# Transposing later batches' attention scores by DMA in 16-bit halves, with a rearranged start, in a cross-covariance attention and MLP kernel

**Chip, cores, metric.** One NeuronCore of a Trainium2 chip. The metric is the device time of one execution in microseconds (us).

## The reference

```python
B, N, C = (4, 6080, 256)                      # q, k, v: fp32
qn = q / (np.linalg.norm(q, axis=1, keepdims=True) + 1e-06)
kn = k / (np.linalg.norm(k, axis=1, keepdims=True) + 1e-06)
s = kn.transpose(0, 2, 1) @ qn / tau           # 256 x 256 a batch
a = softmax(s, axis=-1)                        # (cut)
x = (v @ a).reshape(B * N, C)                  # 24320 x 256
h = x @ w_in                                   # w_in: 256 x 2048
out = gelu_tanh(h) @ w_out                     # w_out: 2048 x 256
```

The kernel folds `a @ w_in` into one matrix `aw` a batch. After that each row of `v` goes through `hp = v @ aw`, a gelu and `yp = g @ w_out`.

## The kernel before

A batch is 12 blocks of up to 512 rows, and a block is 8 steps, called slots here: so 96 slots a batch. In a slot TensorE makes four `hp` products and, after the first block, six to eight `yp` products of the block before. VectorE copies finished `yp` from PSUM, TensorE's output memory, to the tile `ysb`; this copy is called an eviction here. The attention of the next batch is fed in between as a generator, one piece a slot:

```python
for blk in range(n_blocks):
    vT = vT_of.pop(nb)
    turn_v(nb + 2)          # SyncE: transposes v of block nb+2 by DMA, 4 transposes of 64 KB
    load_v(nb + 3)          # GpSimd: loads v of block nb+3, casting fp32 to bf16
    for i in range(NP):     # NP = 8 slots
        # 4 products hp <- vT, aw ; gelu on ScalarE ; yp products of the block before
        next(fill, None)    # a piece of the next batch's attention
```

The generator ends each batch with the part that the change touches. Every `yield` ends a slot:

```python
norms(r)
Gs = scaled(G, r)           # VectorE, 128 x 2 x 256 fp32, scores with k's side scaled
yield
yield
T = turned(Gs)              # TensorE: 4 fp32 transposes into PSUM
# ... (cut) th = tanh(T * rh) on ScalarE, then per half jc:
for jc in range(2):
    yield
    # VectorE: den = 1 - th; den = 1 / den; eT = (1 + th) * den   = exp
yield
yield
rsinv = row_sums(eT)        # TensorE "rs", then a reciprocal on VectorE
for fs in range(D // 512):
    for ic in range(2):
        aw_part(eT, rsinv, aw_next, fs, ic)
        yield
```

Before the main loop the weights are loaded by SyncE and cast by GpSimd, with the loads of v for blocks 1 and 2 among them:

```python
for half in range(2):
    # ... (cut) w_in half: DMA, two casts
    load_v(1 + half)
for half in range(2):
    # w_out half: DMA, one cast (1.9 us)
```

Of the kernel before, what the change touches and what calls it, by code (L numbers as in the profile page):

```python
# [7 lines left out]

FP32 = mybir.dt.float32
BF16 = mybir.dt.bfloat16  # L10
AF = mybir.ActivationFunctionType
ALU = mybir.AluOpType
EPS = 1e-6
# [5 lines left out]
def kernel(  # L19
# [10 lines left out]
    nc = tc.nc  # L30
# [19 lines left out]
    split = ctx.enter_context(tc.tile_pool(name="split", bufs=1))  # L50
    accp = ctx.enter_context(tc.tile_pool(name="accp", bufs=1))
    smx = ctx.enter_context(tc.tile_pool(name="smx", bufs=2))
# [40 lines left out]
    n_all = S_ALL + 1  # L93


    first_chunks = chunks_of([12, 12, 5, 6, 4, 4, 2, 2], 2)
    TAIL, SHARED = 4, 6
    fillers = [0, 0, 5, 7, 4, 3, 1, 0]
    staged = []

    def halves(pool, tag, dtype, size, most=SMAX):
# [27 lines left out]
    ident = const.tile([128, 128], FP32)  # L129
# [68 lines left out]
                                 rhs=ident, is_transpose=True)  # L198
        return T

    def row_sums(eT):
        rs = pA.tile([128, 512], FP32, tag="a", name="rs")
        for ic in range(2):
            for jc in range(2):
                nc.tensor.matmul(
                    rs[:, ic : ic + 1],
                    lhsT=eT[:, jc, ic * 128 : ic * 128 + 128],
                    rhs=ones_bf,
                    start=jc == 0, stop=jc == 1)
        rsinv = smx.tile([128, 2], FP32, tag="rsinv", name="rsinv")  # L210
        nc.vector.reciprocal(rsinv, rs[:, 0:2])
        return rsinv
# [43 lines left out]
    for n, ch in enumerate(first_chunks):  # L256
        st, whole = staged[n]
        size = ch[1]
        qkb, qk_whole = halves(qkp, "qk", BF16, size)
        sqb, sq_whole = halves(sqp, "sq", BF16, size)  # L260
        hi = size + ch[2]
        if whole is None:
            todo = list(zip(qkb, sqb, st))
        else:
            todo = [[y[:, :, 0:hi] for y in (qk_whole, sq_whole, whole)]]
        for to, sq, x in todo:
            nc.vector.tensor_copy(to, x)  # L267
            if n != n_chunks - 2:
                nc.scalar.activation(sq, x, AF.Square)  # L269
        if n == n_chunks - 2:  # L270
            nc.scalar.activation(sqb[1][:, 0:hi], st[1][:, 0:hi], AF.Square)
            nc.vector.tensor_mul(sqb[0][:, 0:hi], qkb[0][:, 0:hi], qkb[0][:, 0:hi])
        keep_clock(fillers[n])
        for s, rows in slots_of(ch, 128):
            gram(G, qkb, s, rows, seen == 0, seen == n_all - 1)
            seen += 1
        if waiting is not None:
            pairs_of(*waiting)
            waiting = None
        if n < 2:  # L280
            pairs_of(n, sqb)
        elif n < TAIL:
            waiting = (n, sqb)
        else:
            sums_of([[y[:rows, s, :] for y in sqb] for s, rows in slots_of(ch, 128)], n == n_chunks - 1)

        for x in ((2, 3) if n == 0 else (4, 5) if n == 1 else (n + 4,)):
            stage_chunk(x)

    v0 = stage.tile([128, 2, SMAX, 256], FP32, tag="st", name="v0")  # L290
# [58 lines left out]
    for half in range(2):  # L349
        w = flat_stage(2)  # L350
        for x in range(2):
            c0 = half * 1024 + x * 512
            nc.sync.dma_start(out=w[:, :, x * 512 : x * 512 + 512], in_=win_v[:, :, c0 : c0 + 512])
            nc.gpsimd.tensor_copy(win_bf[:, :, c0 : c0 + 512], w[:, :, x * 512 : x * 512 + 512])
        load_v(1 + half)
    for half in range(2):
        w = flat_stage(8)
        nc.sync.dma_start(out=w, in_=wout_v[:, half * 8 : half * 8 + 8, :])
        nc.gpsimd.tensor_copy(wout_bf[:, half * 8 : half * 8 + 8, :], w)  # L359


    r = smx.tile([128, 4], FP32, tag="r", name="r")
# [3 lines left out]
    Gs = scaled(G, r)  # L366
# [6 lines left out]
                             rhs=ident, is_transpose=True)  # L373
        vps.append(p)
    keep_clock(1, pY, "y")
    T = turned(Gs)
    keep_clock(1, pY, "y")
    vT0 = vts.tile([128, 2, 512], BF16, tag="vT", name="vT")
    nc.vector.tensor_copy(vT0[:, 0, :], vps[0])
    eT = smx.tile([128, 2, 256], BF16, tag="eT", name="eT")  # L380
    aw = awp.tile([128, 2, D], BF16, tag="aw", name="aw")
    for jc in range(2):
        nc.scalar.activation(eT[:, jc, :], T[:, jc, :], AF.Exp, scale=r[:, jc : jc + 1])  # L383
    nc.scalar.activation(vT0[:, 1, :], vps[1], AF.Copy)


    firsts = []

    def first_aw(n, jc, pool=pY, tag="y"):

        if jc == 0:
            firsts.append(pool.tile([128, 512], FP32, tag=tag, name="ps"))
        nc.tensor.matmul(
            firsts[n][:, 0:256],
            lhsT=eT[:, jc, n % 2 * 128 : n % 2 * 128 + 128],
            rhs=win_bf[:, jc, n // 2 * 256 : n // 2 * 256 + 256],
            start=jc == 0, stop=jc == 1)

    first_aw(0, 0)
    first_aw(1, 0)  # L400
    rsinv = row_sums(eT)
    first_aw(0, 1)
    first_aw(1, 1)
    for n in (2, 3):
        first_aw(n, 0, pA, "a")
        first_aw(n, 1)
    for n in range(4):
        ic, lo = n % 2, n // 2 * 256
# [3 lines left out]
        else:  # L412
            nc.vector.tensor_scalar_mul(dst, firsts[n][:, 0:256], scale)  # L413
    nc.scalar.activation(dummy, ones_f, AF.Gelu_apprx_tanh)
    aw_left = [(fs, ic, *((pA, "a") if fs == 2 else (pY, "y"))) for fs in range(1, 4) for ic in range(2)]

    def more_aw(n):
        for _ in range(n):
# [18 lines left out]
    def attention_steps(b, aw_next):  # L437

        for n in range(16):
            if n in (3, 9):  # L440
                load_qk(b, n // 6)
            if b == 1 and n == 5:
                turn_v_on_pe(1)
            yield
        G = pA.tile([128, 2, 256], FP32, tag="a", name="G")
        acc = accp.tile([128, 2, 256], FP32, tag="acc", name="acc")
        seen = 0
        for n, ch in enumerate(later_chunks):
            load_qk(b, n + 2)
            qk, whole = loaded_of.pop((b, n))  # L450
            for s, rows in slots_of(ch, 128):
                first, last = seen == 0, seen == n_all - 1
                gram(G, qk, s, rows, first, last)
                flat = whole[:rows, :, s, :]
                if first:
                    nc.vector.tensor_mul(acc, flat, flat)
                else:
                    sq = sq1.tile([128, 2, 256], BF16, tag="sq", name="sq")
                    nc.vector.tensor_mul(sq[:rows], flat, flat)  # L459
                    nc.vector.tensor_add(acc[:rows], acc[:rows], sq[:rows])  # L460
                seen += 1
                yield
                if seen % 8 == 0:
                    yield


        parts = [split.tile([128, 2, 256], BF16, tag=f"part{n}", name="part") for n in range(3)]
        nc.vector.tensor_copy(parts[0], acc)
        nc.vector.tensor_sub(acc, acc, parts[0])
        nc.vector.tensor_copy(parts[1], acc)  # L470
        nc.vector.tensor_sub(parts[2], acc, parts[1])
        yield
        yield
        cols = pA.tile([128, 512], FP32, tag="a", name="cols")
        for n, part in enumerate(parts):
            col_sums(cols, [part[:, x] for x in range(2)], ones_bf, n == 0, n == 2)
        r = smx.tile([128, 4], FP32, tag="r", name="r")
        nc.vector.tensor_copy(r, cols[:, 0:4])  # L478
        nc.gpsimd.tensor_tensor(r, r, half4, op=ALU.pow)  # L479
# [4 lines that stand above are left out]
        rh = smx.tile([128, 2], FP32, tag="rh", name="rh")  # L484
        nc.vector.tensor_scalar_mul(rh, r[:, 0:2], 0.5)
        Gs = scaled(G, r)
        yield
        yield
        T = turned(Gs)
        eT = smx.tile([128, 2, 256], BF16, tag="eT", name="eT")  # L490
        if abs(inv_tau) > TANH_MAX:
            for jc in range(2):
                nc.scalar.activation(eT[:, jc, :], T[:, jc, :], AF.Exp, scale=r[:, jc : jc + 1])
            yield
        else:
            th = smx.tile([128, 2, 256], FP32, tag="th", name="th")
            den = smx.tile([128, 2, 256], FP32, tag="den", name="den")
            for jc in range(2):
                nc.scalar.activation(th[:, jc, :], T[:, jc, :], AF.Tanh, scale=rh[:, jc : jc + 1])
            for jc in range(2):  # L500
                yield
                nc.vector.tensor_scalar(den[:, jc, :], th[:, jc, :], -1.0, 1.0,
                                        op0=ALU.mult, op1=ALU.add)
                nc.vector.reciprocal(den[:, jc, :], den[:, jc, :])
                nc.vector.scalar_tensor_tensor(
                    out=eT[:, jc, :], in0=th[:, jc, :], scalar=1.0, in1=den[:, jc, :],
                    op0=ALU.add, op1=ALU.mult)
            yield
            yield
        rsinv = row_sums(eT)  # L510
# [4 lines that stand above are left out]
# [159 lines left out]
```

## Time and profile before

| | before |
|---|---|
| time, median of the runs beside the changed kernel | 753.86 us (753.45 to 754.20, 6 runs) |
| span of the profiled run | 752.0 us |
| TensorE busy | 726.4 us, 97% |
| wait for the first chunk of q and k | 15.8 us |
| TensorE's other waits, all together | 1.7 us |

TensorE is the bound from the moment that batch 0's `aw` is ready (first `hp` at 40.06 us) to the end. A line of the order of time has start, length, engine, source line, operation, output and inputs, count; in brackets the idle time before it and what ended it. In the names, `G` are the products of k and q (the scores), `Gs` the scaled and `T` the transposed scores, `th`, `den` and `eT` the steps of the exponential, `rs` its row sums, `vb` and `vT` a block of v as loaded and transposed. The lines of the page and of the waits are in the prediction below.

### The profile page before, as it was taken

The page shows a single profiled execution, that of the slowest core. Times are in us where ns is not written, and L with a number is a line of the kernel's source. Part 1 is how long each engine was busy: PE and PEld are TensorE (multiplying, and loading weights), DVE is VectorE, ACT ScalarE, POOL GpSimd, SP SyncE. Part 2 cuts the span into 40 slices and gives each one's busy share as a digit, 9 for nine tenths or more (in the row PEclk, how much of TensorE's full clock was granted, in tenths as well). Part 3 has the DMA queues.
Part 4 walks back from the last instruction along what each step waited for, and adds up shares of the span by engine and source line. Part 5 has one row for each costly group of instructions (what it writes and reads, how often), then busy time and mean ns, then how long its engine had stood idle before and what let it go on. Part 6 is the DMA issues. An engine that isn't in the chain of part 4 may idle for free.

```text
span 752.0 us, 12341 instructions
## 1 busy us (share of the span) xinstructions
PE 726.4 (97%) x5186; PEld 502.3 (67%) x5274; DVE 284.3 (38%) x497; ACT 420.3 (56%) x411; POOL 80.8 (11%) x154
## 2 busy tenths in 40 slices
PE   2899999999999999999999999999999999999998
PEld 1656766776666766776666666776666666666666
DVE  3733556463501646554521265555351011011011
ACT  4875555556456555555555555555645655555552
POOL 1061111101012102101001102010101000000000
PEclk9999999999999999999999999999999999999999
DMA  9989685613237685824325876671413533322111
GB/s 369 400 205 200 104 150 139 132 43 69 70 72 144 114 163 108 164 63 75 71 57 117 141 119 124 150 143 46 69 43 85 105 85 70 69 75 54 41 57 57
DMA packets 80183, 85.69 MB, mean 114 GB/s; under 512 B 55424, under 2 KB 59136, under 8 KB 79616
## 3 DMA queue, kind: packets, MB, share of 16 engines
q0 software_dynamic: 14480, 30.87, 25.7%
q1 hardware_dynamic: 65344, 52.39, 24.4%
q10 hardware_dynamic: 304, 1.64, 0.5%
q8 instruction: 41, 0.67, 0.4%
q14 instruction: 14, 0.11, 0.0%
HBM read 78.91 MB, written 24.90 MB: 138 GB/s over the span
## 4 chain that ended last, share of the span: by engine, by line
PE 94%; DMA 3%; ACT 1%; issue 1%; DVE 0%; POOL 0%; SPq 0%; DVEq 0%; POOLq 0%
PE yp L528 44%; PE hp L602 43%; PE G L158 4%; PE ps L218 2%; ACT sq L269 1%; DMA st<-in_q_dram 1%; DMA st<-in_k_dram 1%; PE T L196 0%; POOL wout_bf L359 0%; PE yp L633 0%; PE cols L170 0%; DVE qk L267 0%; DVE aw L413 0%; DVE Gs L188 0%; ACT eT L383 0%
## 5 line engine op out<-in xcount | busy, mean ns | idle before, releaser
L606 ACT ACTIVATE g<-hp 128x1024 bf16<-128x1024 f32 (+1 forms) x384 | 389.8, 1015 | 307.0 <-PE hp L602 295.2
L528 PE MATMUL yp<-wout_bf,g 128*128 128x256 bf16 x3024 | 392.0, 273 | 1.6 <-POOL wout_bf L359 0.7
L602 PE MATMUL hp<-vT,aw 128*128 128x512 bf16 (+1 forms) x1456 | 383.9, 377 | 3.8 <-DVE aw L413 0.2
L528 PEld LDWEIGHTS <-g 128*128 128x128 bf16 x3024 | 295.9, 98 | 114.3 <-issue 1.2
L602 PEld LDWEIGHTS <-aw 128*128 128x128 bf16 x1536 | 149.9, 98 | 104.1 <-DVE aw L413 0.5
L545 DVE COPY ysb<-yp 128x512 f32<-128x512 f32 (+1 forms) x95 | 64.9, 683 | 396.5 <-PE yp L528 396.5
L460 DVE TENSOR_TENSOR acc<-acc,sq 128x512 f32<-128x512 f32 x141 | 97.6, 692 | 4.8
L459 DVE TENSOR_TENSOR sq<-qkb 128x512 bf16<-128x512 bf16 x141 | 58.9, 418 | 0.0
L158 PE MATMUL G<-qkb 128*128 128x256 bf16 x288 | 55.0, 273 | 0.0
L307 POOL DMA_DIRECT2D vb<-in_v_dram x47 | 25.9, 552 | 88.6 <-DMA vT<-vb 81.3
L227 DVE TENSOR_SCALAR aw<-ps,rsinv 128x512 bf16<-128x512 f32 x30 | 22.4, 749 | 23.5 <-PE ps L218 18.3
L158 PEld LDWEIGHTS <-qkb 128*128 128x128 bf16 x288 | 28.2, 98 | 3.3
L332 POOL CAST gate<-g 1x1 f32<-1x1 bf16 x24 | 5.9, 245 | 227.8 <-ACT g L606 227.8
L158 PE MATMUL G<-qk 128*128 128x256 bf16 x96 | 13.5, 298 | 15.8 <-DVE qk L267 15.8
L269 ACT ACTIVATE sq<-st 128x3072 bf16<-128x3072 f32 (+2 forms) x9 | 21.1, 2379 | 11.1 <-DMA st<-in_q_dram 8.2
L158 PEld LDWEIGHTS <-qk 128*128 128x128 bf16 x96 | 9.8, 106 | 19.1 <-DVE qk L267 16.6
L267 DVE CAST qk<-st 128x3072 bf16<-128x3072 f32 (+2 forms) x10 | 14.2, 1438 | 13.1 <-DMA st<-in_q_dram 10.0
L218 PE MATMUL ps<-win_bf,eT 128*128 128x512 bf16 x54 | 16.4, 379 | 0.2
L479 POOL TENSOR_TENSOR r<-r,half 128x4 f32<-128x4 f32 x3 | 3.1, 1042 | 103.4 <-DVE r L478 103.4
L82 POOL DMA_DIRECT2D qkb<-in_q_dram x24 | 12.9, 537 | 5.8 <-issue 4.3
L585 POOL COPY g<-gr 128x1024 bf16<-128x1024 bf16 x2 | 2.1, 1036 | 101.3 <-PE yp L528 101.3
L82 POOL DMA_DIRECT2D qkb<-in_k_dram x24 | 12.9, 539 | 0.0
(73 smaller groups left out, 109.0 us busy)
## 6 DMA issues: line engine op xcount, KB each, us to landing
out_dram<-ysb SPq DMA_DIRECT2D x44, 512.0 KB, 3.0
vb<-in_v_dram POOLq DMA_DIRECT2D x43, 256.0 KB, 6.2
qkb<-in_q_dram POOLq DMA_DIRECT2D x21, 384.0 KB, 4.6
qkb<-in_k_dram POOLq DMA_DIRECT2D x21, 384.0 KB, 6.4
st<-in_q_dram SPq DMA_DIRECT2D x2, 1536.0 KB, 11.8
vT<-vb SPq DMA_TRANSPOSE x184, 3.0
wst<-in_moe_w_in_dram SPq DMA_DIRECT2D x4, 512.0 KB, 7.5
wst<-in_moe_w_out_dram SPq DMA_DIRECT2D x2, 1024.0 KB, 11.7
```

The lines of the kernel that those rows point to most:

```text
L82: engines[x].dma_start(out=dst[x][:, 0:size, :], in_=src[b, s0 * 128 : (s0 + size) * 128, :].rearrange("(p s) c -> p s c", s=size))
L158: nc.tensor.matmul(G[:, ic, :], lhsT=qk[1][:rows, s, ic * 128 : ic * 128 + 128], rhs=qk[0][:rows, s, :], start=first and ic == 0, stop=las ...
L218: nc.tensor.matmul(ps, lhsT=eT[:, jc, ic * 128 : ic * 128 + 128], rhs=win_bf[:, jc, fs * 512 : fs * 512 + 512], start=jc == 0, stop=jc == 1)
L227: nc.vector.tensor_scalar_mul(dst, ps, scale)
L269: nc.scalar.activation(sq, x, AF.Square)
L307: nc.gpsimd.dma_start(out=t[:, 0:n, :], in_=v_rows[r0 : r0 + n * 128, :].rearrange("(p s) c -> p s c", s=n))
L459: nc.vector.tensor_mul(sq[:rows], flat, flat)
L460: nc.vector.tensor_add(acc[:rows], acc[:rows], sq[:rows])
L528: nc.tensor.matmul(yp[:rows, at, :], lhsT=g[:, fc, s * 128 : s * 128 + rows], rhs=wout_bf[:, fc, :], start=fc == 0, stop=fc == FC - 1)
L545: nc.vector.tensor_copy(ysb[:, s0 : s + 1, :], yp[:, 0 : s + 1 - s0, :])
L602: nc.tensor.matmul(hp[:, j, :cols], lhsT=aw[:, cc, fc * 128 : fc * 128 + 128], rhs=vT[:, cc, :cols], start=cc == 0, stop=cc == 1)
L606: nc.scalar.activation(g[:, 2 * i : 2 * i + 2, :cols], hp[:, :, :cols], AF.Gelu_apprx_tanh)
```

## The change

The intent is to take the fp32 transposes of the scores of batches 1 to 3 off TensorE, to start the first products earlier, and to let w_out arrive before v of block 2. `first_chunks` are the pieces in which q and k of batch 0 are loaded, in units of 128 rows; `fillers` counts useless products ahead of each piece, which keep TensorE busy. The core of the diff:

```diff
-    first_chunks = chunks_of([12, 12, 5, 6, 4, 4, 2, 2], 2)
-    TAIL, SHARED = 4, 6
-    fillers = [0, 0, 5, 7, 4, 3, 1, 0]
+    first_chunks = chunks_of([2, 12, 12, 5, 6, 4, 2, 2, 2], 3)
+    TAIL, SHARED = 4, 7
+    fillers = [0, 0, 0, 5, 7, 4, 1, 1, 0]
@@ (cut: other PSUM pools for batch 0's row sums and first products; its T in two tiles)
-        load_v(1 + half)
+        if half == 0:
+            load_v(1)
     for half in range(2):
         w = flat_stage(8)
         nc.sync.dma_start(out=w, in_=wout_v[:, half * 8 : half * 8 + 8, :])
         nc.gpsimd.tensor_copy(wout_bf[:, half * 8 : half * 8 + 8, :], w)
+    load_v(2)
@@ (in the generator)
-        yield
-        yield
-        T = turned(Gs)
+        apart = split.tile([128, 2, 2, 256], U16, tag="apart", name="apart")
+        crossed = split.tile([128, 2, 2, 256], U16, tag="crossed", name="crossed")
+        T = split.tile([128, 2, 256], FP32, tag="T", name="T")
+        bits = Gs.bitcast(U16).rearrange("p a (j h) -> p h a j", h=2)
+        for h in range(2):
+            nc.vector.tensor_copy(apart[:, h], bits[:, h])
+            for ic in range(2):
+                nc.sync.dma_start_transpose(
+                    out=crossed[:, h, :, ic * 128 : ic * 128 + 128], in_=apart[:, h, ic, :])
+        for _ in range(6):
+            yield
+        bits = T.bitcast(U16).rearrange("p a (i h) -> p h a i", h=2)
+        for h in range(2):
+            nc.vector.tensor_copy(bits[:, h], crossed[:, h])
+        yield
```

More of the change, by code (lines that the diff above doesn't have):

```diff
@@ L10 @@
 BF16 = mybir.dt.bfloat16
+U16 = mybir.dt.uint16
 AF = mybir.ActivationFunctionType
@@ L199, in turned, with row_sums @@
         return T
-    def row_sums(eT):
-        rs = pA.tile([128, 512], FP32, tag="a", name="rs")
+    def row_sums(eT, rs=None):
+        if rs is None:
+            rs = pA.tile([128, 512], FP32, tag="a", name="rs")
         for ic in range(2):
@@ L267 @@
             nc.vector.tensor_copy(to, x)
-            if n != n_chunks - 2:
+            if n not in (n_chunks - 3, n_chunks - 2):
                 nc.scalar.activation(sq, x, AF.Square)
-        if n == n_chunks - 2:
+        if n in (n_chunks - 3, n_chunks - 2):
             nc.scalar.activation(sqb[1][:, 0:hi], st[1][:, 0:hi], AF.Square)
@@ L279 @@
             waiting = None
-        if n < 2:
+        if n < 3:
             pairs_of(n, sqb)
@@ L285 @@
             sums_of([[y[:rows, s, :] for y in sqb] for s, rows in slots_of(ch, 128)], n == n_chunks - 1)
-        for x in ((2, 3) if n == 0 else (4, 5) if n == 1 else (n + 4,)):
+        for x in ((2,) if n == 0 else (3, 4) if n == 1 else (5, 6) if n == 2 else (n + 4,)):
             stage_chunk(x)
@@ L375 @@
     keep_clock(1, pY, "y")
-    T = turned(Gs)
-    keep_clock(1, pY, "y")
+    T = [pY.tile([128, 512], FP32, tag="y", name="T") for _ in range(2)]
+    for ic in range(2):
+        for jc in range(2):
+            nc.tensor.matmul(T[jc][:, ic * 128 : ic * 128 + 128],
+                             lhsT=Gs[:, ic, jc * 128 : jc * 128 + 128],
+                             rhs=ident, is_transpose=True)
     vT0 = vts.tile([128, 2, 512], BF16, tag="vT", name="vT")
@@ L382, with first_aw @@
     for jc in range(2):
-        nc.scalar.activation(eT[:, jc, :], T[:, jc, :], AF.Exp, scale=r[:, jc : jc + 1])
+        nc.scalar.activation(eT[:, jc, :], T[jc][:, 0:256], AF.Exp, scale=r[:, jc : jc + 1])
     nc.scalar.activation(vT0[:, 1, :], vps[1], AF.Copy)
     firsts = []
-    def first_aw(n, jc, pool=pY, tag="y"):
+    def first_aw(n, jc, pool=pA, tag="a"):
         if jc == 0:
@@ L400 @@
     first_aw(1, 0)
-    rsinv = row_sums(eT)
+    rsinv = row_sums(eT, pH.tile([128, 2, 512], FP32, tag="h", name="rs")[:, 0, :])
     first_aw(0, 1)
@@ L404 @@
     for n in (2, 3):
-        first_aw(n, 0, pA, "a")
+        first_aw(n, 0, pY, "y")
         first_aw(n, 1)
@@ L414 @@
     nc.scalar.activation(dummy, ones_f, AF.Gelu_apprx_tanh)
-    aw_left = [(fs, ic, *((pA, "a") if fs == 2 else (pY, "y"))) for fs in range(1, 4) for ic in range(2)]
+    aw_left = [(fs, ic, *((pA, "a") if fs == 1 else (pY, "y") if fs == 2 else (pA, "a"))) for fs in range(1, 4) for ic in range(2)]
     def more_aw(n):
@@ L486, in attention_steps @@
         Gs = scaled(G, r)
+        apart = split.tile([128, 2, 2, 256], U16, tag="apart", name="apart")
[4 more added lines that the diff above has]
+            nc.vector.tensor_copy(apart[:, h], bits[:, h])
+            for ic in range(2):
+                nc.sync.dma_start_transpose(
[5 more added lines that the diff above has]
+            nc.vector.tensor_copy(bits[:, h], crossed[:, h])
         yield
-        yield
-        T = turned(Gs)
         eT = smx.tile([128, 2, 256], BF16, tag="eT", name="eT")
@@ L495, in attention_steps @@
         else:
-            th = smx.tile([128, 2, 256], FP32, tag="th", name="th")
-            den = smx.tile([128, 2, 256], FP32, tag="den", name="den")
+            th = split.tile([128, 2, 256], FP32, tag="th", name="th")
+            den = split.tile([128, 2, 256], FP32, tag="den", name="den")
             for jc in range(2):
```

## The prediction

> **What bounds the kernel now.** I read the page first (engine shares, slices, costliest groups), then TensorE's waits, then the order of time around the three places that the change touches: the start, the transposes of the scores, and the loads between 36 and 70 us. The page:
>
> ```profile
> PE 726.4 (97%) x5186; PEld 502.3 (67%) x5274; DVE 284.3 (38%) x497; ACT 420.3 (56%) x411; POOL 80.8 (11%) x154
> ...
> PE   2899999999999999999999999999999999999998
> ...
> DMA  9989685613237685824325876671413533322111
> ```
>
> TensorE is full in every slice but the first; the other engines have room. The DMA queues are full in the first three slices (to about 56 us) and then never again for long. TensorE's waits, all of them:
>
> ```profile
> PE G L158 <- DVE qk L267: 15.8, 3, 14.4
> PE yp L528 <- POOL wout_bf L359: 0.7, 1, 0.7
> PE T L196 <- DVE Gs L188: 0.4, 1, 0.4
> PE ps L393 <- ACT eT L383: 0.4, 1, 0.4
> PE hp L602 <- DVE aw L413: 0.2, 1, 0.2
> ```
>
> (Columns: who, on whom, total us, times, longest.) 15.8 us is the wait for the first chunk of q and k; the rest is small. After 52 us TensorE never waits: any TensorE work taken away there is gained one to one, and any new wait there is lost one to one. One step ("slot") of the main loop after the first block is four hp products and eight yp products; one slot of the second batch with the transposes of the scores in it, from the order of time:
>
> ```profile
> 181.56 1.03 PE L602 MATMUL hp<-vT,aw 128*128 128x512 bf16 x4
> ...
> 183.30 0.60 PE L196 MATMUL T<-ident,Gs 128*128 128x128 f32 x4
> ...
> 183.73 1.03 PE L602 MATMUL hp<-vT,aw 128*128 128x512 bf16 x3
> ...
> 185.47 1.03 PE L602 MATMUL hp<-vT,aw 128*128 128x512 bf16 x4
> ```
>
> From hp to hp it is 183.73-181.56 = 2.17 us with the four transposes and 185.47-183.73 = 1.74 without: they cost 0.43 us a batch, less than their busy time of 0.60, which overlaps.
>
> The first phase, to 34 us, is the load of q and k of batch 0 (2 x 6080 x 256 x 4 bytes = 12.45 MB) at the 400 GB/s of the slices; the windows of 2 us show the DMA share at 0.96 or more from 4 us to 48 us. The start of the steady part:
>
> ```profile
> 48.90 13.50 SPq L321 DMA_TRANSPOSE vT<-vb  x8
> ...
> 49.88 1.90 POOL L359 CAST wout_bf<-wst 128x2048 bf16<-128x2048 f32 x1 [2.02 <-PE hp L602]
> ...
> 51.72 0.54 POOL L307 DMA_DIRECT2D vb<-in_v_dram  x1
> ```
>
> GpSimd casts the second half of w_out at 49.88, and TensorE waits 0.7 us for it. The queue of SyncE transposes v of block 2 from 48.90 on (four transposes, 1.3 us each to issue), then v of block 3. Last, what a transpose by DMA takes from issue to landing, for those issued in 48 to 50.5 us, and in 57 to 62 us:
>
> ```profile
> vT<-vb SPq DMA_TRANSPOSE x2, 2.4
> ```
>
> ```profile
> vb<-in_v_dram POOLq DMA_DIRECT2D x3, 256.0 KB, 8.6
> ...
> vT<-vb SPq DMA_TRANSPOSE x4, 9.1
> ```
>
> The same 64 KB transposes take 2.4 us on an idle queue and 9.1 when GpSimd's casting loads are in flight. Over the whole run the median is 3.0.
>
> **What the Trainium skill says.** "DMA: Bandwidth & Descriptors", section "DMA Transpose (X-bar)": a transpose by DMA is for 2-byte types and is issued from SyncE or ScalarE only. Hence the split of the fp32 scores into upper and lower halves; the trace has v transposed this way from SyncE, 184 times. The same page, "Issuing engines are not separate DMA queues": DMAs of all issuers run on the same 16 engines and interleave. The trace agrees, with the 2.4 us that become 9.1. "TensorE: Matmul & The Clock Gate", Part 1: about 3.4 us without work put TensorE's clock back to half, and it takes as long to recover. The trace of before shows the recovery after the first wait: 24 G products took 4.50 us at 14.38, the next 24 took 2.79 us, a loss of 1.7.
>
> **The change part by part.**
>
> 1. Chunks 2, 12, 12, 5, 6, 4, 2, 2, 2 instead of 12, 12, 5, 6, 4, 4, 2, 2. The first squares and products start at about 5 us instead of 10.9 and 14.4. This gains nothing: the last k chunk (issued 25.61, in use at 34.4) lands when 12.45 MB have passed a full queue. ScalarE squares 1.5 MB in 2.75 us, faster than the 3.75 us that they take to arrive, so no backlog is worked off either. I put 0, at most 0.3 either way.
>
> 2. Scores of batch 0 in two PSUM tiles, first products and row sums in other pools. The exponential of the first half need not wait for the last transpose: about (0.74-0.27)/3 = 0.16 us. The row sums no longer share a pool with the first products, which hides little. Gain 0.15.
>
> 3. The load of v for block 2 goes behind the casts of w_out. Its 0.52 MB no longer compete with w_out: 0.52 MB at 400 GB/s = 1.3 us. The second half of w_out (issued 36.91, 12.9 us to landing, so 49.8) comes at 48.5, and its cast ends at 50.4 instead of 51.8. TensorE's wait of 0.7 us goes, and 0.2 of an earlier one. Gain 0.9. But the load of that v, issued at 42.68 and landed 6.2 us later (48.9), is now issued at 50.4. See rival A.
>
> 4. Batches 1 to 3: four fp32 transposes less on TensorE: 3 x 0.43 = 1.3 us gained. In their place VectorE makes 4 copies of 512 16-bit elements a batch, at 0.43 to 0.69 us (casts and copies of 128x512 in the trace), and SyncE issues 4 transposes at 1.3 us. Timing for batch 1: scaled scores ready at 182.0, the two halves split at 182.5 and 183, transposes issued at 182.5 to 187.7, while SyncE has nothing else until 188. No load is in flight (the next is after 204), so the last lands 2.4 us after its issue, near 189. Six slots of 1.74 after slot 75 VectorE gets to the merge, at 188 to 190; it waits a microsecond at most, and its next eviction is due at 191 or later. Off the path. Everything behind it shifts by five slots, and the last aw product goes from step 89 to step 94 of 96, so it still fits before the batch ends.
>
> Sum without anything new: -0.15 - 0.9 - 1.3 = -2.35, so 751.5 us.
>
> **The rivals.**
>
> A: a new wait, for v of block 2. The v load issued at 50.4 takes at least the 4.0 us of the fastest such load seen (at 176.06), so its transposes are issued at 54.4, 55.7, 56.9, 58.2. By then the loads of v of blocks 3 to 5 and of the first two chunks of q and k are in flight. In before, a transpose issued at 52.81 with fewer of them took 8.7 us, the four at 57.36 to 61.15 a median of 9.6, and the v load at 57.88 took 11.1 and landed at 69.0. With one load more in the same stretch, I estimate the fourth transpose to land between 67 and 70. Block 2's first hp ran at 64.84 in before and is due at 64.84 - 1.05 = 63.8. TensorE would stand for some 3 to 6 us, once. If it stands for over 3.4 us, the clock falls and costs about 1.7 more. Middle: 5 + 1.7 - 2.35 = +4.4, so 758 us. For it: every transpose of before that was issued in loaded stretches landed late. Against it: whoever tuned the kernel moved this load on purpose, and if these transposes go ahead of the backlog (2.4 us each) the last lands at 60.6 and nothing waits.
>
> B: the merge blocks VectorE. If the score transposes land late, VectorE stands at the merge, yp evictions are late and TensorE with them. Before shows 5.4 us for a transpose beside two v loads (176.5), but those loads land before 182. At most 1 us a batch: 754 without A.
>
> C: the gain is hidden altogether, because the slot is bound by something else than TensorE. Against it: ScalarE needs 1.02 us of the 1.74, and the weight loads 1.61 of the 2.17. I give it 5%.
>
> D: the two-slot chunks' smaller descriptors (2 KB) slow the first phase, or the clock is lower at its end because fillers moved: at most +0.5.
>
> **Range and chances.** Rival A with 0.65, centred at 758 with 755 to 761; without it 751.5, give or take 0.7. The middle of the mixture is near 756.5; 8 in 10 from 750.9 to 761. The 2% marks are 738.8 and 769: neither is within reach of any sum above, so within 2% has 0.97, faster 0.01, slower 0.02.
>
> **What would show it.** Right: in the waits of TensorE a new line hp <- DMA vT, once, some 3 to 6 us long, near 64 us; before it the wait on wout_bf is gone; slots of batches 1 to 3 all 1.74 without a 2.17 from transposes; the score transposes at 2.4 to 3 us to landing; first squares at 5 us but the last k chunk still in use at 34.4. Wrong: no wait on vT (then 751.5 holds), a wait of yp on evictions in slots 81 to 83 of a batch (rival B), or the last chunk landing off 34.3 by over half a microsecond.

## The result

The changed kernel is correct and takes 761.47 us (median of 6 runs, 760.22 to 764.77) against 753.86. The ratio is 1.0104 (95% interval 1.0084 to 1.0124). Here and below a ratio is the mean time of one kernel's fast runs over that of the other's fast runs of the same rounds, so it is not quite the ratio of the medians quoted.

The page of the changed kernel (engine shares; then busy tenths in 40 slices of 19 us, with TensorE's granted clock in the last row):

```profile
span 759.8 us, 12450 instructions
...
PE 733.7 (97%) x5267; PEld 501.7 (66%) x5267; DVE 289.3 (38%) x511; ACT 419.7 (55%) x412; POOL 80.0 (11%) x154
...
PE   3896999999999999999999999999999999999998
...
PEclk9998999999999999999999999999999999999999
```

The fourth slice, 57 to 76 us, has a TensorE digit of 6 and a clock digit of 8. TensorE's waits in the changed kernel, all of them (who, on whom, total us, times, longest):

```profile
PE G L159 <- DVE qk L269: 14.4, 4, 7.2
PE hp L623 <- DMA vT<-vb: 5.8, 1, 5.8
PE rs L207 <- DVE eT L526: 1.4, 3, 0.5
PE ps L401 <- ACT eT L391: 0.5, 1, 0.5
PE hp L623 <- DVE aw L421: 0.2, 1, 0.2
```

Compare them with the five lines in the prediction. The wait on w_out is gone. Two are new: one of 5.8 us on the transposed v, and three of 0.5 us of the row sums `rs` on the exponentials `eT`. The place of the long one, in TensorE's order of time:

```profile
63.09 0.82 PE L549 MATMUL yp<-wout_bf,g 128*128 128x256 bf16 x6
69.73 1.86 PE L623 MATMUL hp<-vT,aw 128*128 128x512 bf16 x4 [5.82 <-DMA vT<-vb]
71.39 1.91 PE L549 MATMUL yp<-wout_bf,g 128*128 128x256 bf16 x8
73.09 0.63 PE L159 MATMUL G<-qkb 128*128 128x256 bf16 x2
73.52 1.41 PE L623 MATMUL hp<-vT,aw 128*128 128x512 bf16 x4
...
75.86 1.03 PE L623 MATMUL hp<-vT,aw 128*128 128x512 bf16 x4
```

The slots after the wait take 73.52 - 69.73 = 3.79 us and 75.86 - 73.52 = 2.34. In before the same slots take 1.96 each (64.84, 66.80, 68.75). That is 2.2 us on top of the wait itself. Four products take 1.86 us where they took 1.03.

What SyncE and GpSimd did before it (SPq is SyncE's queue of DMA issues):

```profile
48.12 1.89 POOL L362 CAST wout_bf<-wst 128x2048 bf16<-128x2048 f32 x1 [2.14 <-DMA wst<-in_moe_w_out_dram]
49.95 1.07 POOL L309 DMA_DIRECT2D vb<-in_v_dram  x2
...
53.79 0.59 POOL L309 DMA_DIRECT2D vb<-in_v_dram  x1
```

```profile
53.72 13.34 SPq L323 DMA_TRANSPOSE vT<-vb  x8
```

The cast of w_out starts at 48.12 instead of 49.88. The transposes of block 2 start at 53.72 instead of 48.90. For the four of block 2, issued from 53.7 to 58.6 us, the view of that tile gives these times from issue to landing:

```profile
DMA to landing us min/median/max: 9.5/11.5/13.0
```

In before the four transposes of block 2 had a median of 4.2 us.

I paired the 384 gelu activations of both traces one by one. The changed kernel is 1.10 us ahead at slot 8, 7.10 behind from slot 17 on, and falls back by 0.18 to 0.19 us in each of the three batches that have score transposes. At the last gelu it is 7.65 behind.

### The profile page after: what moved, and what is told of

Same layout as the page of the kernel before. It is cut to its first block, busy times and chain, and to the rows that moved or that the text cites. A ratio compares the mean times of both kernels' runs of the same rounds, so it can differ in the third digit from the quotient of the medians.

```text
span 759.8 us, 12450 instructions
## 1 busy us (share of the span) xinstructions
PE 733.7 (97%) x5267; PEld 501.7 (66%) x5267; DVE 289.3 (38%) x511; ACT 419.7 (55%) x412; POOL 80.0 (11%) x154
## 4 chain that ended last, share of the span: by engine, by line
PE 88%; DMA 7%; DVE 2%; SPq 1%; ACT 1%; POOL 0%; issue 0%; POOLq 0%; ACTq 0%
PE yp L549 42%; PE hp L623 41%; PE G L159 4%; DMA st<-in_k_dram 4%; DMA vT<-vb 1%; DVE den L525 1%; PE ps L220 1%; DMA wst<-in_moe_w_out_dram 1%; SPq L323 1%; ACT sq L271 1%; DMA vb<-in_v_dram 0%; POOL wout_bf L362 0%; DVE eT L526 0%; DVE ysb L566 0%; PE yp L654 0%
## 5 line engine op out<-in xcount | busy, mean ns | idle before, releaser
L623 PE MATMUL hp<-vT,aw 128*128 128x512 bf16 (+1 forms) x1536 | 392.2, 378 | 6.0 <-DMA vT<-vb 5.8
```

The source lines that it names most:

```text
L623: nc.tensor.matmul(hp[:, j, :cols], lhsT=aw[:, cc, fc * 128 : fc * 128 + 128], rhs=vT[:, cc, :cols], start=cc == 0, stop=cc == 1)
```

## The experiments

The rounds of one call share their runs of the kernel before. Its medians were 754.07 us in the first two calls and 754.45 in the third.

**The theory after the result.** (1) The move of the v load alone makes the stall: its transposes are issued five microseconds later and then land behind GpSimd's casting loads. (2) The slow slots after it are a lowered clock. (3) The score transposes save TensorE 0.43 us a batch, but the exponential's chain now starts behind an eviction of `yp`, and the row sums wait. (I took this eviction to come in every second slot; it comes in every fourth, see e6 and e7.) The rivals: the stall needs the new start; the slow slots have another cause; the row sums wait because the score transposes land late, or as an aftermath of the stall.

### e1: the load's move alone

The kernel before, with this edit:

```diff
-        load_v(1 + half)
+        if half == 0:
+            load_v(1)
 ... (w_out)
+    load_v(2)
```

> The kernel before with one edit alone: the load of v for block 2 is issued behind the casts of w_out. Theory (the load's move makes the late transposes and the stall): one wait of hp on the transposed v of 5 to 6 us near 64 us, about 2 us more of slow products after it, less 0.9 for the wait on w_out that goes: +7 us, so about 761. Rival (the stall comes from the new chunks or pools of the start, or needs them): no such wait, 753 to 754.

Measured: 761.40 us (759.96 to 762.52), ratio 1.0094 (1.0080 to 1.0108). TensorE's waits have the same long line:

```profile
PE hp L604 <- DMA vT<-vb: 6.0, 1, 6.0
```

This one edit carries the whole loss, within the intervals. The rival that the new start is needed falls.

### e2: the score transposes by DMA alone

The kernel before, with the generator's part of the diff and nothing else.

> The kernel before with the score transposes by DMA alone. Theory (1.3 us of TensorE work gone, but 3 x 0.5 us or more of new waits of the row sums on the exponentials): +0.2 a batch, +0.5 in all, about 754.4, with a wait of rs on eT, three times 0.5. Rival (the waits in the changed kernel are an aftermath of the stall at 64 us): -1.3, about 752.6, with no wait of rs on eT.

Measured: 754.64 us (754.41 to 755.20), ratio 1.0008 (0.9994 to 1.0022). TensorE's waits have:

```profile
PE rs L206 <- DVE eT L519: 1.4, 3, 0.5
PE yp L542 <- POOL wout_bf L360: 0.8, 1, 0.8
```

The interval includes no change. But the gain of 1.3 us (0.17%) that I had predicted lies outside it, and the trace has the three waits without any stall at 64 us. So they are no aftermath.

### e3: the start's edits alone

The kernel before, with the new chunks, fillers, PSUM pools and the two tiles for batch 0's scores.

> The kernel before with the start's edits alone: chunk sizes, fillers, PSUM pools, two tiles for the scores of batch 0; neither the load nor the later score transposes. Theory: the last k chunk lands where it did (34.3 us) and only the split tile gains, -0.16 us, so 753.7. Rival (the early start of squares and products gains): -1 us or more.

Measured: 753.80 us (753.40 to 754.88), ratio 0.9996 (0.9983 to 1.0008). The early start gains nothing that can be measured. In this profiled run the first gelu was even 0.73 us later than in before, with a granted clock of 0.79 between 18 and 26 us. By slot 8 nothing of that was left, because the wait on w_out, which is there without the load's move (0.7 us in before, none in this trace), took it up.

### e4: the changed kernel with the load put back

The reverse of e1's edit, on the changed kernel.

> The changed kernel with the load of v for block 2 back in its old place. Theory: the stall and the slow products after it (5.8 and 2.2 us) go, the wait on w_out (0.9) returns: 761.5 - 8.0 + 0.9 = 754.4, so a shade above before because of the scores. Rival (the stall has other causes beside the load): above 756.

Measured: 754.87 us (754.09 to 755.34), ratio 1.0006 (0.9994 to 1.0019). The stall is gone, and the three waits of `rs` remain. e1 and e4 agree: the move is needed and sufficient for the stall.

### e5: products in the stall

```diff
+            if nb == 2:
+                idle = pA.tile([128, 512], FP32, tag="a", name="idle")
+                for _ in range(24):
+                    nc.tensor.matmul(idle, lhsT=filler[:, 0:128], rhs=filler, start=True, stop=True)
             for i in range(NP):
```

> The changed kernel with 24 filler products (about 5.2 us at full clock) on TensorE in the stall, ahead of block 2's first hp, so that TensorE is not idle for long. Theory (the slots after the stall are slow because the idle time lowered the clock): the transposed v lands where it did, the slots after it take 1.96 us at once, and about 2.2 us are saved: 759.3. Rival (the slots after the stall are slow for another reason, such as products or loads that are late): no change, 761.5.

Measured: 759.77 us (759.43 to 761.35), ratio 1.0073 (1.0059 to 1.0087), against 1.0104 for the changed kernel: 0.31% or 2.3 us less. First the changed kernel, then e5, from 63 to 75 us (the third number from the end is the granted clock):

```profile
63.00:75.00 12.00, 6.18 (x29) 3.24 (x27) 3.35 (x6) 2.08 (x3) 1.24 (x3) 0.72 1.14 160
```

```profile
63.00:75.00 12.00, 11.10 (x66) 6.10 (x64) 3.34 (x6) 3.34 (x5) 0.63 (x2) 1.00 1.09 177
```

TensorE's order of time in e5:

```profile
65.49 5.34 PE L620 MATMUL idle<-filler 128*128 128x512 bf16 x24
71.74 1.02 PE L627 MATMUL hp<-vT,aw 128*128 128x512 bf16 x4 [0.90 <-DMA vT<-vb]
...
73.69 1.03 PE L627 MATMUL hp<-vT,aw 128*128 128x512 bf16 x4
```

The useless products filled the wait for v: TensorE was idle for another 0.90 us after them. The clock stayed at 1.00 and the slot behind it took 1.95 us instead of 3.79. So the second part of the loss is the clock.

### e6 and e7: the merge one slot earlier, one slot later

Both are e4 with one number changed:

```diff
-        for _ in range(6):
+        for _ in range(5):        # e6;   range(7) in e7
             yield
```

> The changed kernel with the load back, and the merge of the score halves after 5 slots instead of 6. Theory (the exponential's chain starts behind an eviction of yp, which falls in every second slot, so an odd shift of the chain against before costs half a slot): no wait of rs on eT, -1.4 us against the load put back alone, about 752.9. Rival (the score transposes land too late for the merge): the wait of rs stays or grows, 754.4 or more.

> The changed kernel with the load back, and the merge after 7 slots. Theory (every second slot): no wait of rs on eT either, the same about 752.9 as with 5 slots. Rival (late landing of the score transposes): better than with 5 slots. If 5 waits and 7 does not, the landing was the cause.

Measured: e6 752.58 us (752.35 to 753.35), ratio 0.9980 (0.9967 to 0.9993); e7 752.62 (752.43 to 752.91), ratio 0.9979 (0.9966 to 0.9991). Neither has a wait of `rs` on `eT`. With e4 at 1.0006, one slot in either direction is worth 0.26%, 2 us. Late landing would have made 5 slots worse than 6. The view of the halves in the changed kernel excludes it too:

```profile
L503 SPq DMA_TRANSPOSE crossed<-apart x12: 1167/1216/1245, 189.6 to 553.3; - x12
...
DMA to landing us min/median/max: 2.3/2.3/2.3
```

All twelve land in 2.3 us. How the chain stands against the eviction, batch 1, in before (tanh, the first half's `den` at once, then the eviction `ysb` between the halves, then `rs`):

```profile
183.94 0.84 ACT L499 ACTIVATE th<-T,rh 128x256 f32<-128x256 f32 x2 [0.29 <-PE T L196]
184.44 0.29 DVE L502 TENSOR_SCALAR den<-th 128x256 f32<-128x256 f32 x1 [2.46 <-ACT th L499]
...
187.41 0.69 DVE L545 COPY ysb<-yp 128x512 f32<-128x512 f32 x1 [0.43 <-PE yp L528]
...
190.12 0.42 DVE L505 SCALAR_TENSOR_TENSOR eT<-th,den 128x256 bf16<-128x256 f32 x1
190.68 0.24 PE L205 MATMUL rs<-ones_bf,eT 128*128 128x1 bf16 x4
```

And in the changed kernel:

```profile
199.33 0.89 ACT L520 ACTIVATE th<-T,rh 128x256 f32<-128x256 f32 x2
...
201.02 0.69 DVE L566 COPY ysb<-yp 128x512 f32<-128x512 f32 x1 [4.76 <-PE yp L549]
201.63 0.28 DVE L523 TENSOR_SCALAR den<-th 128x256 f32<-128x256 f32 x1
...
206.03 0.17 PE L207 MATMUL rs<-ones_bf,eT 128*128 128x1 bf16 x1
206.19 0.42 DVE L526 SCALAR_TENSOR_TENSOR eT<-th,den 128x256 bf16<-128x256 f32 x1
206.67 0.23 PE L207 MATMUL rs<-ones_bf,eT 128*128 128x1 bf16 x3 [0.47 <-DVE eT L526]
```

In before VectorE takes up the first `den` 0.5 us after tanh began, works while `yp` is being made, and has the second `eT` ready at 190.54, with almost nothing to spare before `rs` (190.68). In the changed kernel the first `den` starts only 2.3 us after tanh began, because VectorE stands first in an eviction that TensorE has not finished (idle for 4.76 us, then 0.69 of work). The chain of two times 0.28 + 1.75 + 0.43 us then ends 0.5 us after the row sums want it.

I had expected this of every odd shift, with an eviction in every second slot. The traces say otherwise: evictions start at 187.13, 194.07 and 201.02 us in the changed kernel, 6.9 us or four slots of 1.74 apart, and the trace has 95 of them for 384 slots. The change shifted the chain by five slots, one more than this period. e6 shifts it by four, and it meets the eviction as before: between the halves. e7 shifts it by six, and it does not:

```profile
194.23 0.69 DVE L564 COPY ysb<-yp 128x512 f32<-128x512 f32 x1 [4.76 <-PE yp L547]
...
194.84 0.28 DVE L521 TENSOR_SCALAR den<-th 128x256 f32<-128x256 f32 x1
...
199.40 0.42 DVE L524 SCALAR_TENSOR_TENSOR eT<-th,den 128x256 bf16<-128x256 f32 x1
...
200.97 0.24 PE L207 MATMUL rs<-ones_bf,eT 128*128 128x1 bf16 x4
```

The chain starts behind the eviction just as in the changed kernel (4.76 us idle again), but `rs` comes one slot later, and `eT` is ready 1.15 us before it. So e6 avoids the eviction, and e7 leaves time for it. `range(8)` was not run. Paired by gelu activations as above, e6 and e7 each gain 0.44 us a batch on before, which is what the transposes had cost TensorE; e4 loses 0.18.

### e8: block 2's v transposed on TensorE

```diff
             if b == 1 and n == 5:
                 turn_v_on_pe(1)
+            if b == 1 and n == 13:
+                turn_v_on_pe(2)
@@
-            turn_v(nb + 2)
+            if nb > 0:
+                turn_v(nb + 2)
```

> The changed kernel, its late load of v for block 2 kept, but that v transposed on TensorE (8 bf16 transposes, 0.43 us, as block 1's v is) and not by DMA. Theory (the load itself lands in time at about 54 us; it is the transposes by DMA behind the other loads that are late): no stall, 761.5 - 8.0 + 0.43 = 753.9. Rival (the load lands too late): TensorE waits for it, well above 754.

Measured: 754.66 us (753.81 to 755.85), ratio 1.0009 (0.9996 to 1.0021), with no wait on v at all. So the late load itself is in time. Only its transposes by DMA are late.

### e9: GpSimd's later loads held until the transposes have landed

```diff
             if at_slot:
                 pace()
+            if (b, n) == (1, 1):
+                nc.gpsimd.tensor_copy(gate[:, 2:6], vT_of[2][0:1, 0, 127:512:128])
```

> The changed kernel, late load and late transposes kept, but GpSimd holds its loads of the second chunk of q and k and of v for block 5 until the four transposes of block 2's v have landed (a tiny copy reads one element of each). Theory (a transpose by DMA lands behind the casting loads that are in flight, not behind some other queue): with those loads held the last transpose lands at 64 us or earlier, the stall falls from 5.8 to at most 1 us, 753.5 to 754.5. Rival (four transposes behind the first loads alone are as late, or the held loads are missed later by the products): a stall of 4 us or more stays, or a new wait of G on q and k appears; above 757.

Measured: 755.08 us (753.88 to 755.77), ratio 1.0008 (0.9995 to 1.0020). No wait on v, no new wait of G. The four transposes, issued at the same place as in the changed kernel:

```profile
DMA to landing us min/median/max: 4.5/6.4/8.5
```

They took 9.5/11.5/13.0 in the changed kernel. With two loads of q and k and one of v less in flight they land five microseconds sooner, and TensorE finds them. So the casting loads in flight set when a transpose lands. The landings of the single DMAs show it too: in the changed kernel the last of these loads lands at 68.94 us and the last three transposes at 68.93, 69.26 and 69.59; in e9 the last load lands at 62.28 and the four at 62.62, 62.92, 63.23 and 63.55. The median is a little above my expectation of 753.5 to 754.5; the first hp of this profiled run was late, as in e3, which the load's move leaves uncovered.

### e10 and e11: the parts that help

e10 is the kernel before with the PSUM pools of the start, the score transposes and `range(7)`: old chunks, old place of the load. e11 is e10 with the load moved and e9's hold.

> The kernel before with the PSUM pools of the start, the score transposes by DMA and the merge after 7 slots: neither the new chunks nor the load's move. Theory (the scores save 1.3 once the wait of the row sums is gone, the pools 0.16, and the new chunks give nothing or cost up to 0.8 where the clock dips at 18 to 26 us): 752.4, clock 1.00 in 18 to 26 us, 0 to 0.5 better than the run with the new chunks and 7 slots. Rival (the new chunks help): 753 or more.

> As the run with the old chunks and 7 slots, and with the load moved behind w_out and GpSimd's later loads held. Theory: the wait on w_out (0.9) goes and the hold keeps the stall away: 751.5, the fastest so far. Rival: the stall is only partly away, 752.4 or more.

Measured: e10 752.73 us (752.50 to 754.42), ratio 0.9984 (0.9970 to 0.9997); e11 751.92 (751.68 to 753.36), ratio 0.9970 (0.9957 to 0.9982). e11 is the fastest kernel, 2.3 us or 0.3% under before by the ratio. TensorE's waits in e11, all of them:

```profile
PE G L159 <- DVE qk L269: 15.3, 3, 14.4
PE ps L403 <- ACT eT L393: 0.5, 1, 0.5
PE T L385 <- DVE Gs L189: 0.3, 1, 0.3
PE hp L625 <- DVE aw L423: 0.2, 1, 0.2
```

No wait of the main loop is left. e10's and e11's intervals overlap, so that the load's move with the hold gains on its own (0.8 us by the medians) is likely from the trace, where the w_out wait is gone, but not shown by the times.

### e12: fillers in the early idle time

e3 with one number changed, products in the idle time between the first and the second chunk:

```diff
-    fillers = [0, 0, 0, 5, 7, 4, 1, 1, 0]
+    fillers = [0, 16, 0, 5, 7, 4, 1, 1, 0]
```

> The kernel with the start's edits alone, and 16 filler products ahead of the second chunk, in the idle time from 6.5 to 13.7 us. Theory (the early burst at 5 us with 7 us of idle time behind it lets the clock fall again in some executions, seen as a granted clock of 0.79 in 18 to 26 us): clock 1.00 there, first hp 0.7 us earlier than in the profile of the start alone, 753.3 to 753.8. Rival (the dip has no such cause): clock 0.79 stays, no change.

Measured: 754.44 us (753.52 to 754.80), ratio 0.9997 (0.9985 to 1.0010). The expectation failed: the granted clock in 18 to 26 us is again 0.79. The trace shows what these fillers did:

```profile
13.69 2.79 PE L159 MATMUL G<-qk 128*128 128x256 bf16 x24 [1.64 <-DVE qk L269]
...
21.09 4.33 PE L159 MATMUL G<-qk 128*128 128x256 bf16 x24 [4.03 <-DVE qk L269]
```

The second chunk's 24 products ran at full clock (2.79 us, against 5.22 in e3), so TensorE then waited 4.03 us for the third chunk instead of 1.61, and that chunk ran slowly. The longer wait is not shown to be the reason: in e3 the third chunk was as slow (4.37 us) after 1.61. (For the first products the clock column does not help: e3 has 1.00 in 12 to 18 us, where the second chunk took 5.22.) What decides whether the clock dips stays open: the same start had 0.79 in the profiled runs of e3 and e5 to e9, and 1.00 in those of the changed kernel and of e4. Its cost is at most the 0.7 to 1.6 us by which the first gelu was late in those runs. Executions of the kernel before vary in a like way: in the first call three of nine have a mean granted clock of 0.997 and take 754.63 to 755.27 us, the others 0.999 to 1.000 and 753.63 to 754.41.

## Why the prediction was wrong

The time came out at 761.47 us, 0.5 above the range's upper end of 761.0 and 5 above the middle. The step that failed is part 4; in rival A two terms were too small. By the steps of the prediction:

- **Part 1, the chunks (0 gained): right.** e3 shows no change. That a start at 5 us can let the clock dip later was not seen.
- **Part 2, the pools and tiles (0.15): right in size**, 0.16 us at the first gelu of the changed kernel's trace, too small for the times to show.
- **Part 3, the wait on w_out (0.9): right.** The cast came at 48.12, estimated 48.5; at slot 8 the kernel was 1.10 us ahead, predicted 1.05 for parts 2 and 3 together.
- **Rival A, the stall on v of block 2: right in mechanism, place and cause** (e1, e4, e8, e9), but given only 0.65, so the point was a mixture of two outcomes that was neither. I held against it that whoever tuned the kernel had moved the load on purpose. The trace argued for it without exception, more than I saw: I read the DMA queues as full in the first three slices "and then never again for long", but the fourth digit, 56 to 75 us, is a 9 too, and that is where the transposes were late. (The lines with 9.1 us are of issues in 51.6 to 59 us; those in 57 to 62 have 9.6.) The terms: 5 us for the stall measured 5.8, 1.7 us for the clock measured 2.2 (e5).
- **Part 4, the score transposes (1.3 gained, "Off the path"): this step failed.** The 0.43 us a batch did leave TensorE, but a wait of 0.5 us came in, and its knock-on in the slot: +0.18 a batch, +0.5 in all by the paired traces of e2 and of the changed kernel (e2's times, +0.08%, cannot tell it from none). The sum of what goes and what comes was off by 1.8 us. I checked when the transposes land, which was right (2.3 us each), that VectorE would wait about a microsecond at the merge (0.6), and that the work fits before slot 96. I did not check which of VectorE's evictions the exponential's chain would queue behind after a shift by five slots, nor that in before it met `rs` with 0.1 us to spare.
- **Rival B** looked at the eviction behind the merge, the wrong side: not the eviction waits for the chain, the chain waits for the eviction (e6, e7). **Rivals C and D**: C did not happen; e6 and e7 gain what TensorE is spared. D's half microsecond was not seen in the times of e3.

Had rival A stood alone with its sizes, the sum was 753.86 + 5 + 1.7 - 2.35 = 758.2. Of the remaining 3.3 us, part 4 (1.8), the stall (0.8) and the clock (0.5) explain 3.1. The other 1.7 us up from the middle of 756.5 were lost by mixing this sum with the one without a stall.

## What to carry to other kernels

When a transfer is moved behind another, look at what is in flight at its new time: a small transpose by DMA took 2.3 us on an idle queue and 9.5 to 13 behind casting loads. On an engine that is saturated, a wait of several microseconds is paid once for itself and once more for the clock (5.8 us, then 2.2; in e1 6.0, then 2.3); filling it with useless products is a cheap test of that. When work shifts by some steps in a software pipeline, check the steps' periodic work on each in-order engine, here an eviction in every fourth step, and how much time the reader of the result has left: one step more or less turned no gain into one of 1.5 us (0.2%).

## What the Trainium skill lacked or had wrong

- "DMA: Bandwidth & Descriptors", "Queues, rings and completion order", has each DMA engine go round robin between queues, packet by packet, which no run here shows by itself. It has no figure for how a small transfer of SyncE's queue fares beside casting loads of GpSimd's. The runs: 64 KB transposes land in 2.3 us alone, in 9.5 to 13.0 us when five to eight loads are in flight at their issue, and in 4.5 to 8.5 when three loads are held back and four or five are in flight (e9).
- The same page, "DMA Transpose (X-bar)", says that it takes 2-byte types only, which the kernel's split agrees with. It does not say that fp32 can go through it as two 16-bit halves. The runs: correct results, four transposes of 2.3 us and four VectorE copies of 0.42 to 0.46 us for 256 x 256.
- "TensorE: Matmul & The Clock Gate", Part 4, gives a PE transpose of 128 x 128 bf16 at about 275 ns in one kernel. Here the record of an fp32 one is 273 ns too, but the page does not say what a transpose adds to a full stream: four cost 0.43 us, 0.11 each.
- The same page, Part 1, gives idle windows of about 3.4 us, and what 32 gaps cost one kernel together, but no measured cost of a single gap. The runs: a wait of 5.8 us cost 2.2 us more in the two slots behind it, and nothing more when it was filled with products (e5). After a burst at 5 us and 7 us of idle time the clock dipped again at 18 to 26 us in some executions and not in others. The page says that its windows run freely and do not reset when a kernel starts, which could make executions differ; no run here tests that.
